# Pooled attention and feed-forward: softmax normalisation of a head pair's two steps in joint instructions of 576 columns

## The chip, the cores and the metric

The kernel runs on one core of one Trainium2 chip. The metric is the device time of one execution in microseconds (us), as the median of the runs. Engines are named as in the profile: PE is TensorE, PEld its weight loads, DVE VectorE, ACT ScalarE, POOL GpSimd, SP SyncE (DMA issue only).

## What is computed

Attention with the queries pooled by two, and then a feed-forward network on its output. In the reference (fp32; B 4, H 8, S 1152, D 64; 2304 tokens, model width 512, hidden width 2048), shortened:

```python
q_pool = q.reshape(B, H, S // 2, 2, D).mean(axis=3)
scores = np.matmul(q_pool, k.transpose(0, 1, 3, 2)) / np.sqrt(D)
scores = scores - np.max(scores, axis=-1, keepdims=True)
attn = np.exp(scores)
attn = attn / (np.sum(attn, axis=-1, keepdims=True) + 1e-09)
x = np.matmul(attn, v)            # heads side by side: 2304 x 512
h = x @ w_in
sp = np.log1p(np.exp(np.minimum(h, 20.0)))   # h itself where h > 20
out = (h * np.tanh(sp)) @ w_out
```

## The kernel before

The attention runs in 32 steps. A step is one batch, one pair of heads and one half of the pooled queries: 2 heads x 288 queries = 576 columns. Two steps that follow each other, an even and an odd one, are the two halves of the same head pair; "a pair" below means these two steps, 16 pairs in all. The keys are cut into nine chunks of 128. The work of several steps overlaps: one step's scores are made while an earlier step's exponentials and still earlier steps' normalisations are done.

In a step, QK (L164) makes the scores of a chunk in PSUM (tile `s`, two buffers), CP (L174, ScalarE) copies them to SBUF (`TA`, `TB`), MX and MXF (L185, L189, VectorE) take a running maximum (`rmax`). MT, TMAX and MB (L200, L206, L217) turn it into one maximum per query, spread over all partitions; SUB (L223, VectorE) subtracts it, EXP (L227, ScalarE) exponentiates. PV (L246) multiplies with the values into the PSUM tile `pv`, of which there is one; PVE (L257, ScalarE) copies it to SBUF (`pvs`), and the next step's first PV waits for that copy. For the denominator, ADD (L232 to L238) sums the exponentials of the chunks on GpSimd, three chunks of them by a DMA that adds (L236, `acc<-TB`), and FIN0 (L268) sums over the partitions with a matrix of ones into the PSUM tile `Sb`, whose value stands in all partitions.

The normalisation, which the change touches, follows, for steps 0 to 29, on 288 columns (each head on its 64 partitions). With s the sum: FLN (L273, ScalarE) makes ln(s), FEX (L276, ScalarE) r = exp(-ln s), FC (L280, ScalarE) e = -s, FE (L284, GpSimd) e = e r, FT (L288, ScalarE) e = 2 + e, which is one Newton step on r, FU (L299, GpSimd) `pvs` = `pvs` r, and FX (L303, GpSimd) writes e times `pvs` to `xT`, the input of the feed-forward part. Steps 30 and 31 are normalised by VectorE instead (LX).

The order of the instructions is written out by hand: tables FILL, STEP, PAIR and EDGE give each action a time, and the program sorts by it. STEP has one time for even and one for odd steps, counted in steps after the step's own start; FILL and EDGE hold those of the first and the last steps. An engine works through its instructions in this order and waits at each for its operands and its buffer. The rows of STEP for the actions of the change:

```python
            (FC, 3.4059, 3.6027),
            (FLN, 3.4296, 3.4470),
            (FEX, 3.5419, 3.4904),
            (FE, 3.6257, 3.7684),
            (FU, 4.1203, 3.8913),
            (FT, 4.3117, 3.9096),
            (FX, 4.8298, 4.4442),
```

The feed-forward part starts as the attention ends, at about 423 us, and holds TensorE until the end.

Of the kernel before, what the change touches and what calls it, by code (L numbers as in the profile page):

```python
# [8 lines left out]
F32 = mybir.dt.float32  # L9
# [3 lines left out]
AF = mybir.ActivationFunctionType  # L13
ALU = mybir.AluOpType
# [9 lines left out]
def tile_pooled_attention_then_winograd_ffn(ctx: ExitStack, tc: tile.TileContext, q, k, v, moe_w_in, moe_w_out, out, outT):  # L24
    nc = tc.nc
    B, H, S, D = SHAPE
    SQ = S // 2
    NT, DM = B * SQ, out.shape[1]
    DFF = moe_w_out.shape[0]
    P = 128  # L30
# [3 lines left out]
    HQ = SQ // 2  # L34
# [15 lines left out]
    pe, dve, act, pool, sp = nc.tensor, nc.vector, nc.scalar, nc.gpsimd, nc.sync  # L50
# [4 lines left out]
    one, eps = (cst[:, n:n + 1] for n in range(2))  # L55
    xT = const.tile([P, NP, NT], F32, name="xT")

    steps = [(b, hp, hf) for b in range(B) for hp in range(NP) for hf in range(2)]
# [4 lines left out]
    def open_pool(name, bufs, side="left", space=bass.MemoryType.SB):  # L63
        shut[name] = ExitStack()
        pools[name] = shut[name].enter_context(
            tc.tile_pool(name=name, bufs=bufs, side=side, space=space, reuse_waits="tile")
        )
        return pools[name]
# [3 lines left out]
    if True:  # L72
# [7 lines left out]

        p1 = open_pool("p1", 1)
        p2 = open_pool("p2", 2)
        p3 = open_pool("p3", 3)
        pqk = open_pool("pqk", 2)
        pre = open_pool("pre", 1)
        wraw_p = open_pool("wraw", 2, side="right")
# [63 lines left out]
        rmaxs, Mbs, pvs, pvn, accs = {}, {}, {}, {}, {}  # L150
# [89 lines left out]
        def PV(i, c):  # L240
# [4 lines left out]
            for j in range(2):  # L245
# [5 lines left out]
                    stop=(pvn[i] == NC),  # L251
                )

        def PVE(i):
            ps = pvs[i]
            pvs[i] = p3.tile([P, HQ], F32, tag="pvs", name=f"pvs{i}")
            act.copy(pvs[i], ps[:, 0:HQ])  # L257

        fin = {}

# [8 lines left out]
            fin[i] = Sb[:, 0:HQ]  # L269

        def FLN(i):
            fin[i, "r"] = p2.tile([P, HQ], F32, tag="rs", name=f"rs{i}")
            act.activation(fin[i, "r"], fin[i], AF.Ln, bias=eps)  # L273

        def FEX(i):
            act.activation(fin[i, "r"], fin[i, "r"], AF.Exp, scale=-1.0)  # L276

        def FC(i):
            fin[i, "e"] = p2.tile([P, HQ], F32, tag="es", name=f"es{i}")
            act.activation(fin[i, "e"], fin[i], AF.Copy, bias=-1e-9, scale=-1.0)  # L280

        def FE(i):
            e = fin[i, "e"]
            pool.tensor_tensor(e, e, fin[i, "r"], ALU.mult)  # L284

        def FT(i):
            e = fin[i, "e"]
            act.activation(e, e, AF.Copy, bias=2.0, scale=1.0)  # L288

        def LX(i):  # L290

            b, hp, hf = steps[i]
            r = p2.tile([P, HQ], F32, tag="rs", name=f"rs{i}")
            dve.tensor_scalar(r, fin.pop(i), 1e-9, None, ALU.add)
            dve.reciprocal(r, r)
            dve.tensor_tensor(xT[:, hp, b * SQ + hf * HQ:b * SQ + (hf + 1) * HQ], r, pvs.pop(i), ALU.mult)

        def FU(i):
            pool.tensor_tensor(pvs[i], pvs[i], fin[i, "r"], ALU.mult)  # L299

        def FX(i):
            b, hp, hf = steps[i]
            pool.tensor_tensor(  # L303
                xT[:, hp, b * SQ + hf * HQ:b * SQ + (hf + 1) * HQ], fin[i, "e"], pvs.pop(i), ALU.mult
            )

        QHP = (1,)
        pieces = [(2 * fp + j % 2, j // 2) for fp in range(NFP) for j in range(4)]
# [291 lines left out]
        ps, sv = {}, {}  # L600
# [142 lines left out]
        for n, u in enumerate(units):  # L743
            if u[0] == 0:
                banks[u] = ("b", "a", "c") if n % 2 else ("a", "b", "c")
            else:
                x, y, z = banks[units[n - 1]]
# [3 lines left out]
        XD = (0, 1, 2, 3)  # L751
        BYREC = (NS - 2, NS - 1,)
        GONE = [(i, fn) for i in BYREC for fn in (FLN, FEX, FC, FE, FT, FU, FX)]
        def close(*names):
            for n in names:
                shut[n].close()
# [15 lines left out]
            open_pool("ps2", 1, side="right", space=PSUM)  # L772

        def reuse_rest():
            close("p3", "p2", "p1")
            open_pool("wf", 1)
            open_pool("pad", 1).tile([P, 16], F32, name="pad")
            open_pool("xt", 1)
            open_pool("ev", 2)
            open_pool("sx", 2)  # L780
            open_pool("x3", 1)

        def reuse_lead():
# [139 lines left out]
            (2.0890, QK, 2, 6),  # L923
            (2.1220, SUB, 1, 2),
            (2.1370, PVE, 0),
            (2.1370, QK, 2, 7),
            (2.1570, ADD, 1, 0),
# [56 lines left out]
            (3.1610, QK, 3, 7),  # L984
            (3.2030, SUB, 2, 2),
            (3.2062, PVE, 1),
            (3.2157, QK, 3, 8),
            (3.2287, ADD, 2, 0),
# [11 lines left out]
            (3.4400, QK, 4, 0),  # L1000
            (3.4460, ADD, 1, 3),
            (3.4540, FLN, 0),
            (3.4840, SUB, 2, 3),
            (3.4960, QK, 4, 1),
            (3.5080, CP, 4, 0),
            (3.5510, FC, 0),
            (3.5510, PV, 2, 4),
            (3.5739, CP, 4, 1),
            (3.6030, QK, 4, 2),
            (3.6170, FEX, 0),  # L1010
            (3.6200, load_k, 3),
            (3.6350, MX, 4, 1),
            (3.6510, MT, 3),
            (3.6650, FE, 0),
            (3.6710, CP, 4, 2),
            (3.7010, QK, 4, 3),
# [28 lines left out]
            (4.1590, QK, 4, 7),  # L1045
            (4.2010, SUB, 3, 2),
            (4.2030, PVE, 2),
            (4.2130, QK, 4, 8),
            (4.2257, CP, 4, 7),
# [3 lines left out]
            (4.3040, MX, 4, 7),  # L1053
            (4.3130, PV, 3, 1),
            (4.3230, FLN, 1),
            (4.3520, PV, 3, 3),
            (4.3550, FC, 1),
            (4.3580, MX, 4, 8),
            (4.3780, EXP, 3, 2),
# [3 lines left out]
            (4.4300, load_q, 4),  # L1063
            (4.4390, QK, 5, 0),
            (4.4650, FEX, 1),
            (4.4820, SUB, 3, 3),
            (4.4930, FU, 0),
            (4.4940, QK, 5, 1),
            (4.5180, CP, 5, 0),
# [20 lines left out]
            (4.9120, QK, 5, 5),  # L1090
            (4.9210, ADD, 2, 4),
            (4.9210, FT, 0),
            (4.9350, MX, 5, 4),
            (4.9450, EXP, 4, 0),
# [6 lines left out]
            (5.0880, CP, 5, 6),  # L1101
            (5.0920, MX, 5, 5),
            (5.1170, FX, 0),
            (5.1192, PV, 3, 8),
            (5.1300, EXP, 4, 1),
            (5.1460, MX, 5, 6),
            (5.1678, QK, 5, 7),
            (5.1790, FE, 1),
            (5.2000, SUB, 4, 2),
            (5.2157, QK, 5, 8),  # L1110
# [20 lines left out]
            (5.5480, PV, 4, 4),  # L1131
            (5.5600, CP, 6, 1),
            (5.5810, FU, 1),
            (5.6000, QK, 6, 2),
            (5.6030, FT, 1),
            (5.6200, load_k, 4),
            (5.6297, MX, 6, 1),
            (5.6460, FX, 1),
            (5.6480, MT, 5),
            (5.6680, CP, 6, 2),  # L1140
# [615 lines left out]
            (10.1622, A_g, 1, 1),  # L1756
            (10.4532, FIN0, 30),
            (10.5378, LX, 30),
            (10.6934, ADD, 31, 3),
            (10.9320, A_gh, 2, 0),  # L1760
# [10 lines left out]
            (13.1756, A_gh, 2, 1),  # L1771
            (13.3311, split_l, 3, 1),
            (13.5491, LX, 31),
            (13.7245, O_, 1, 0),
            (14.2248, reuse_rest),
            (14.3971, XS, 0, "T1"),
            (14.5382, split_l, 4, 3),
# [789 lines left out]
        for u in units:  # L2567
            if 2 <= u[1] <= NFP - 2:
                for t, fn, *a in STEADY[u[0] > 0]:
                    a = (4 * u[1] + a[0], a[1]) if fn is conv else (u, *a)  # L2570
# [46 lines left out]
```

## Time and profile before

| | |
|---|---|
| median of 3 runs | 785.08 us (784.74 to 788.81) |
| profiled execution | 784.51 us, span 782.7 us |
| granted TensorE clock, mean | 0.993 of full speed |
| busy share of the span | PE 98%, DVE 87%, ACT 82%, POOL 84% |
| chain that ended last | PE 86%, DVE 3%, ACT 3%, DMA 3%, POOL 2% |
| attention | about 0 to 423 us |

The span reaches from the first to the last instruction of the profiled execution. An engine's busy share is an average over the attention and the feed-forward part, which have different loads, so the stretches have to be looked at apart. Ends of matrix multiplications are modelled, so a busy PE need not be PE at its peak.

### The profile page before, as it was taken

To read this page: it belongs to the slowest core of one execution; us is meant where nothing else is said; L and a number is where in the kernel's file an instruction comes from. 1 tells how busy PE (TensorE), PEld (TensorE's weight loads), DVE (VectorE), ACT (ScalarE), POOL (GpSimd) and SP (SyncE) were. 2 spreads that over 40 slices of the span, in tenths; PEclk is the share of its full clock that TensorE was granted. 3 is DMA by queue.
4 is the path that set the end of the run, shared out by engine and by line. 5 is a ranking of instruction groups with operands and counts; after the bars stand their busy time and mean duration, and the time that the engine had idled before them with its cause. 6 is when DMAs were issued, how large, how long until landed. Compare 5 with 4: busy or idle time off the path is not lost.

```text
span 782.7 us, 14324 instructions
## 1 busy us (share of the span) xinstructions
PE 767.4 (98%) x5123; PEld 558.1 (71%) x5123; DVE 680.6 (87%) x959; ACT 642.1 (82%) x1110; POOL 654.3 (84%) x505
## 2 busy tenths in 40 slices
PE   7999999999999999999999999999999999999998
PEld 5454555545555454555557988899899999999998
DVE  5999999999999999999976778877778889587876
ACT  6999999999999999999885887777677687877762
POOL 4679988989889898988887598886788899998884
PEclk9899999999999999999999999999999999999999
DMA  7556575565755656455432788874664232254242
GB/s 269 166 152 142 176 176 116 143 151 138 181 111 149 152 137 170 116 148 116 111 69 46 241 277 290 284 257 172 192 210 151 95 121 69 95 172 142 95 132 101
DMA packets 44470, 121.90 MB, mean 156 GB/s; under 512 B 4592, under 2 KB 16368, under 8 KB 44400
## 3 DMA queue, kind: packets, MB, share of 16 engines
q1 hardware_dynamic: 34608, 71.45, 27.5%
q0 software_dynamic: 4608, 28.31, 18.4%
q10 hardware_dynamic: 5184, 21.24, 8.0%
q8 instruction: 40, 0.66, 0.3%
q14 instruction: 30, 0.25, 0.1%
HBM read 70.65 MB, written 22.02 MB: 118 GB/s over the span
## 4 chain that ended last, share of the span: by engine, by line
PE 86%; DVE 3%; ACT 3%; DMA 3%; POOL 2%; issue 1%; SPq 0%; ACTq 0%; DVEq 0%; POOLq 0%
PE s L164 20%; PE pv L246 17%; PE ma L616 11%; PE O L727 8%; PE OAy L678 7%; PE mc L616 6%; PE O L678 6%; PE mb L616 3%; PE Sb L268 2%; DMA acc<-TB 2%; PE mt L200 2%; PE h L433 1%; PE Mb L217 1%; PE OZ L710 1%; POOL acc L238 1%
## 5 line engine op out<-in xcount | busy, mean ns | idle before, releaser
L164 PE MATMUL s<-qT,kT 64*128 64x288 f32 x1152 | 205.4, 454 | 4.0 <-ACT TB L174 1.8
L164 PEld LDWEIGHTS s<-qT,kT 64*128 64x128 f32 x1152 | 94.0, 189 | 99.8 <-DVE rmax L185 24.9
L174 ACT COPY TA<-s 128x576 f32<-128x576 f32 x192 | 117.9, 638 | 22.9 <-PE s L164 16.5
L223 DVE TENSOR_TENSOR TA<-TA,Mb 128x1152 f32<-128x1152 f32 x96 | 128.9, 1347 | 1.9 <-PE Mb L217 1.0
L227 ACT ACTIVATE TA<-TA 128x1152 f32<-128x1152 f32 x96 | 112.8, 1176 | 4.1 <-DVE TA L223 3.6
L246 PE MATMUL pv<-TA,vn 128*64 128x288 f32 x768 | 115.2, 422 | 0.8 <-ACT TA L227 0.8
L232 POOL TENSOR_TENSOR acc<-TA 128x1152 f32<-128x1152 f32 x32 | 85.0, 2656 | 36.2 <-PE s L164 19.1
L185 DVE TENSOR_TENSOR rmax<-s,rmax 128x576 f32<-128x576 f32 x128 | 93.3, 749 | 2.1 <-ACT TB L174 1.8
L238 POOL TENSOR_TENSOR acc<-acc 128x576 f32<-128x576 f32 x64 | 91.9, 1436 | 3.9 <-DMA acc<-TB 2.6
L246 PEld LDWEIGHTS pv<-TA,vn 128*64 128x64 f32 x768 | 47.2, 137 | 48.5 <-issue 9.7
L691 DVE TENSOR_TENSOR xT<-xT,OAy 128x384 f32<-128x384 f32 x104 | 54.7, 548 | 11.9 <-PE OAy L678 11.6
L223 DVE TENSOR_TENSOR TB<-TB,Mb 128x1728 f32<-128x1728 f32 x32 | 62.2, 1944 | 0.0
L246 PE MATMUL pv<-TB,vn 128*64 128x288 f32 x384 | 61.3, 415 | 0.0
L174 ACT COPY TB<-s 128x576 f32<-128x576 f32 x96 | 59.8, 654 | 1.8 <-PE s L164 1.7
L598 POOL TENSOR_TENSOR wbl<-wS,wbh 128x1024 fp32r<-128x1024 f32 x20 | 49.5, 2476 | 5.8 <-ACT wbh L594 5.8
L227 ACT ACTIVATE TB<-TB 128x1728 f32<-128x1728 f32 x32 | 52.7, 1648 | 0.0
L185 DVE TENSOR_TENSOR rmax<-s,TA 128x576 f32<-128x576 f32 x64 | 48.3, 755 | 3.8 <-ACT TA L174 3.7
L234 POOL TENSOR_TENSOR acc<-TA 128x576 f32<-128x576 f32 x32 | 45.6, 1424 | 2.5 <-ACT TA L227 2.3
L246 PEld LDWEIGHTS pv<-TB,vn 128*64 128x64 f32 x384 | 24.0, 136 | 25.2 <-issue 11.9
L598 POOL TENSOR_TENSOR wal<-wS,wah 128x768 fp32r<-128x768 f32 x19 | 36.8, 1936 | 3.3 <-ACT wah L594 3.1
L598 POOL TENSOR_TENSOR woal<-wO,woah 128x1024 fp32r<-128x1024 f32 x13 | 31.4, 2415 | 7.9 <-ACT woah L594 6.4
L620 ACT COPY s<-ma 128x384 f32<-128x384 f32 x44 | 21.2, 482 | 20.2 <-PE ma L616 20.2
(305 smaller groups left out, 2241.3 us busy)
## 6 DMA issues: line engine op xcount, KB each, us to landing
acc<-TB POOLq DMA_DIRECT2D x32, 864.0 KB, 6.4
ri<-in_moe_w_in_dram SPq DMA_DIRECT2D x16, 512.0 KB, 4.6
ro<-in_moe_w_out_dram SPq DMA_DIRECT2D x16, 512.0 KB, 4.2
qn<-in_q_dram ACTq DMA_DIRECT2D x12, 576.0 KB, 5.0
kT<-in_k_dram ACTq DMA_DIRECT2D x12, 576.0 KB, 3.8
vn<-in_v_dram ACTq DMA_DIRECT2D x12, 576.0 KB, 4.1
wS<-sumsh SPq DMA_DIRECT2D x12, 512.0 KB, 4.0
wO<-sumso SPq DMA_DIRECT2D x13, 384.0 KB, 4.4
```

Of the source, the lines that this page charges most:

```text
L164: pe.matmul(s[:, j, 0:HQ], kT[64 * j:64 * j + 64, c], qT[64 * j:64 * j + 64, hf], start=True, stop=True,)
L174: act.copy(T(i, c), ss[i, c])
L185: dve.tensor_tensor(ss[i, c] if c == FOLD else r, ss[i, c], x, ALU.max)
L223: dve.tensor_tensor(x, x, Mbs[i].unsqueeze(1).to_broadcast([P, w, W]), ALU.subtract)
L227: act.activation(x, x, AF.Exp, scale=0.0625)
L232: pool.tensor_tensor(accs[i][:, 0:2], T(i, 0, 2), T(i, 2, 4), ALU.add)
L238: pool.tensor_tensor(accs[i][:, 0], accs[i][:, 0], accs[i][:, n - 2], ALU.add)
L246: pe.matmul(pvs[i][64 * j:64 * j + 64, 0:HQ], vn[:, j, c, :], T(i, c)[:, j], start=(pvn[i] == 1), stop=(pvn[i] == NC),)
L598: (dve if e == "dve" else pool).tensor_tensor(l, w_part(u, q), f32(h), ALU.subtract)
L616: pe.matmul(o, a, b, start=(new and m == 0), stop=(last and m == len(seq) - 1), skip_group_check=True)
L678: pe.matmul(o, x, y, start=(n == 0 and i not in CHAIN_O[1:]), stop=(n == 2 and i not in CHAIN_O[:3]), skip_group_check=True)
L727: pe.matmul(o, x, y[:, f], start=(f == 0 and m == 0), stop=(f == 1 and m == 2))
```

## The change

Instead of one tile of 288 columns for each step, `pvs`, `rs` and `es` become tiles of 2 x 288 columns for each pair; `half_of` picks a step's half. PVE, FLN and FC still run for each step and write their half. FEX, FE, FT, FU and FX run only for the odd step of a pair, on all 576 columns, and do nothing for the even step. The tables are the same, so the joint instruction stands where the odd step's stood. `pvs` had three buffers of one step and has two of a pair now; `rs` and `es` had two of one step and have two of a pair. 15 pairs are normalised so: 15 x 3 products of GpSimd and 15 x 2 operations of ScalarE fall away, and as many are twice as long.

```diff
-        p3 = open_pool("p3", 3)
...
+        def half_of(x, i):
+            return x[i // 2][:, i % 2]
+
+        pvx, rsx, esx = {}, {}, {}
+
         def PVE(i):
-            ps = pvs[i]
-            pvs[i] = p3.tile([P, HQ], F32, tag="pvs", name=f"pvs{i}")
-            act.copy(pvs[i], ps[:, 0:HQ])
+            ps = pvs.pop(i)
+            if i // 2 not in pvx:
+                pvx[i // 2] = p2.tile([P, 2, HQ], F32, tag="pvs", name=f"pvs{i // 2}")
+            act.copy(half_of(pvx, i), ps[:, 0:HQ])
...
         def FLN(i):
-            fin[i, "r"] = p2.tile([P, HQ], F32, tag="rs", name=f"rs{i}")
-            act.activation(fin[i, "r"], fin[i], AF.Ln, bias=eps)
+            if i // 2 not in rsx:
+                rsx[i // 2] = p2.tile([P, 2, HQ], F32, tag="rs", name=f"rs{i // 2}")
+            act.activation(half_of(rsx, i), fin[i], AF.Ln, bias=eps)
+
+        def FC(i):
+            if i // 2 not in esx:
+                esx[i // 2] = p2.tile([P, 2, HQ], F32, tag="es", name=f"es{i // 2}")
+            act.activation(half_of(esx, i), fin[i], AF.Copy, bias=-1e-9, scale=-1.0)
 
         def FEX(i):
-            act.activation(fin[i, "r"], fin[i, "r"], AF.Exp, scale=-1.0)
-
-        def FC(i):
-            fin[i, "e"] = p2.tile([P, HQ], F32, tag="es", name=f"es{i}")
-            act.activation(fin[i, "e"], fin[i], AF.Copy, bias=-1e-9, scale=-1.0)
+            if i % 2:
+                r = rsx[i // 2]
+                act.activation(r, r, AF.Exp, scale=-1.0)
 
         def FE(i):
-            e = fin[i, "e"]
-            pool.tensor_tensor(e, e, fin[i, "r"], ALU.mult)
+            if i % 2:
+                e = esx[i // 2]
+                pool.tensor_tensor(e, e, rsx[i // 2], ALU.mult)
 
         def FT(i):
-            e = fin[i, "e"]
-            act.activation(e, e, AF.Copy, bias=2.0, scale=1.0)
+            if i % 2:
+                e = esx[i // 2]
+                act.activation(e, e, AF.Copy, bias=2.0, scale=1.0)
+
+        def FU(i):
+            if i % 2:
+                x = pvx[i // 2]
+                pool.tensor_tensor(x, x, rsx[i // 2], ALU.mult)
+
+        def FX(i):
+            if i % 2:
+                b, hp, _ = steps[i]
+                x = xT[:, hp, b * SQ:(b + 1) * SQ].rearrange("p (a b) -> p a b", a=2)
+                pool.tensor_tensor(x, esx.pop(i // 2), pvx.pop(i // 2), ALU.mult)
```

The order of TensorE's and of VectorE's instructions is the same before and after. GpSimd's, first: a stretch from the middle of the attention, from a step's first sum of exponentials (L232) to the DMA sum (L236). The line numbers of the changed kernel differ: L284, L303 and L299 of before are FE, FX and FU, and L294, L310 and L304 are the same after; the last row but one is the sum that FIN0 waits for. Before:

```order
L232 TENSOR_TENSOR acc_2409<-TA_158 128x1152
L238 TENSOR_TENSOR acc_2289<-acc_2289 128x576
L234 TENSOR_TENSOR acc_2409<-TA_158 128x576
L284 TENSOR_TENSOR es_2449<-es_2449,rs_2434 128x288
L303 TENSOR_TENSOR xT<-es_2305,pvs_2154 128x288
L299 TENSOR_TENSOR pvs_2284<-pvs_2284,rs_2434 128x288
L238 TENSOR_TENSOR acc_2289<-acc_2289 128x576
L236 DMA acc_2409<-TB_159 128x1728
```

The same stretch after:

```order
L231 TENSOR_TENSOR acc_2580<-TA_155 128x1152
L237 TENSOR_TENSOR acc_2463<-acc_2463 128x576
L233 TENSOR_TENSOR acc_2580<-TA_155 128x576
L294 TENSOR_TENSOR es_2479<-es_2479,rs_2482 128x576
L304 TENSOR_TENSOR pvs_2334<-pvs_2334,rs_2482 128x576
L237 TENSOR_TENSOR acc_2463<-acc_2463 128x576
L235 DMA acc_2580<-TB_156 128x1728
```

FE and FU are an odd step's and have become joint; FX was an even step's and is gone from here. In the other step of the pair, FX is the joint one and FE and FU are gone.

ScalarE's, second: from an odd step's FT (L288 before, L299 after) to PVE (L257 before, L262 after), the copy that frees `pv`. Before:

```order
L288 ACTIVATE es_3659<-es_3659 128x288
L227 ACTIVATE TA_158<-TA_158 128x1152
L174 COPY TA_158<-s_5_3706 128x576
L174 COPY TB_159<-s_6_3717 128x576
L227 ACTIVATE TA_158<-TA_158 128x1152
L257 COPY pvs_3736<-pv_3621 128x288
```

After:

```order
L299 ACTIVATE es_3415<-es_3415 128x576
L226 ACTIVATE TA_155<-TA_155 128x1152
L173 COPY TA_155<-s_5_3599 128x576
L173 COPY TB_156<-s_6_3610 128x576
L226 ACTIVATE TA_155<-TA_155 128x1152
L262 COPY pvs_3504<-pv_3518 128x288
```

Nothing has moved here; FT has 576 columns instead of 288, and PVE, still of one step, comes behind it.

## Rows read from the trace of the kernel before

**Rows 1.** Busy us of each engine in one stretch, clock, DMA.

```profile
core 0: us, PE busy (x) PEld busy (x) DVE busy (x) ACT busy (x) POOL busy (x), PEclk, DMA share, GB/s
200.00:240.00 40.00, 40.00 (x313) 20.82 (x311) 39.29 (x42) 37.49 (x62) 36.03 (x30) 1.00 0.60 156
```

**Rows 2.** Waits, 40 to 400 us: total us, times, longest.

```profile
PEld s L164 <- DVE rmax L185: 22.5, 56, 0.6
...
POOL acc L232 <- ACT TA L227: 14.6, 12, 1.5
```

**Rows 3.** Chain of work that ended last: start us, us, engine, output, line.

```profile
198.03 2.09 PE pv L246 x16
...
222.63 2.09 PE pv L246 x16
```

**Rows 4.** Instructions by line and shape, 0 to 405 us: busy us, mean ns.

```profile
L174 ACT COPY TA<-s 128x576 f32<-128x576 f32 x192 | 117.9, 638 | 22.9 <-PE s L164 16.5 <-POOL xT L303 4.2 <-DVE rmax L185 1.9
...
L227 ACT ACTIVATE TA<-TA 128x1152 f32<-128x1152 f32 x93 | 109.3, 1177 | 2.1 <-DVE TA L223 1.8
...
L227 ACT ACTIVATE TB<-TB 128x1728 f32<-128x1728 f32 x31 | 51.1, 1648 | 0.0
...
L138 POOL TENSOR_TENSOR qT<-qn 128x576 f32<-128x576 f32 x15 | 25.4, 1695 | 1.8 <-DMA qn<-in_q_dram 1.8
...
L276 ACT ACTIVATE rs<-rs 128x288 f32<-128x288 f32 x30 | 13.4, 447 | 0.4
L288 ACT ACTIVATE es<-es 128x288 f32<-128x288 f32 x28 | 12.9, 462 | 0.0
```

**Rows 5.** Timeline of GpSimd, tight step: start us, us, instruction.

```profile
214.08 1.42 POOL L234 TENSOR_TENSOR acc<-TA 128x576 f32<-128x576 f32 x1
215.46 0.79 POOL L284 TENSOR_TENSOR es<-es,rs 128x288 f32<-128x288 f32 x1
216.21 0.80 POOL L303 TENSOR_TENSOR xT<-es,pvs 128x288 f32<-128x288 f32 x1
216.97 0.80 POOL L299 TENSOR_TENSOR pvs<-pvs,rs 128x288 f32<-128x288 f32 x1
217.73 1.41 POOL L238 TENSOR_TENSOR acc<-acc 128x576 f32<-128x576 f32 x1
```

**Rows 6.** Timeline of all engines, same step: Sb, PVE and pv.

```profile
220.11 0.20 PEld L268 LDWEIGHTS Sb<-acc,cst 128*64 128x64 f32 x4 [0.38 <-issue]
...
221.83 0.42 ACT L257 COPY pvs<-pv 128x288 f32<-128x288 f32 x1
...
222.56 0.44 PEld L246 LDWEIGHTS pv<-TA,vn 128*64 128x64 f32 x6 [0.39 <-ACT pvs L257]
```

**Rows 7.** Timeline of GpSimd and TensorE, steps 3 to 6; the page's DMA issues.

```profile
78.52 0.80 POOL L299 TENSOR_TENSOR pvs<-pvs,rs 128x288 f32<-128x288 f32 x1
79.56 0.80 POOL L303 TENSOR_TENSOR xT<-es,pvs 128x288 f32<-128x288 f32 x1 [0.24 <-ACT es L288]
...
83.17 0.88 POOL L236 DMA_DIRECT2D acc<-TB  x1
...
90.41 1.41 POOL L238 TENSOR_TENSOR acc<-acc 128x576 f32<-128x576 f32 x1
...
94.66 1.41 POOL L238 TENSOR_TENSOR acc<-acc 128x576 f32<-128x576 f32 x1
...
97.08 0.71 PE L268 MATMUL Sb<-acc,cst 128*64 128x288 f32 x4
...
acc<-TB POOLq DMA_DIRECT2D x32, 864.0 KB, 6.4
```

**Rows 8.** Timeline of GpSimd and TensorE around one late DMA.

```profile
337.34 1.42 POOL L238 TENSOR_TENSOR acc<-acc 128x576 f32<-128x576 f32 x1 [1.57 <-DMA acc<-TB]
...
343.82 0.70 PE L268 MATMUL Sb<-acc,cst 128*64 128x288 f32 x4 [0.63 <-POOL acc L238]
```

**Rows 9.** Chain of work that ended last, end of the attention.

```profile
393.55 0.33 ACT es L288
...
407.98 0.67 ACT es L288 x2
```

More of the change, by code (lines that the diff above doesn't have):

```diff
@@ L290, in LX @@
         def LX(i):
             b, hp, hf = steps[i]
-            r = p2.tile([P, HQ], F32, tag="rs", name=f"rs{i}")
+            if i // 2 not in rsx:
+                rsx[i // 2] = p2.tile([P, 2, HQ], F32, tag="rs", name=f"rs{i // 2}")
+            r = half_of(rsx, i)
             dve.tensor_scalar(r, fin.pop(i), 1e-9, None, ALU.add)
             dve.reciprocal(r, r)
-            dve.tensor_tensor(xT[:, hp, b * SQ + hf * HQ:b * SQ + (hf + 1) * HQ], r, pvs.pop(i), ALU.mult)
-        def FU(i):
-            pool.tensor_tensor(pvs[i], pvs[i], fin[i, "r"], ALU.mult)
@@ L301, in FX @@
[L301 to L305, printed above, removed]
+            dve.tensor_tensor(xT[:, hp, b * SQ + hf * HQ:b * SQ + (hf + 1) * HQ], r, half_of(pvx, i), ALU.mult)
         QHP = (1,)
@@ L774, in reuse_rest @@
         def reuse_rest():
-            close("p3", "p2", "p1")
+            close("p2", "p1")
             open_pool("wf", 1)
```

## The prediction

> **What bounds the kernel now.** I read four views in this order: busy time by stretches, the waits, the chain of work that ended last, and the timeline around the products that the change touches. They have to answer one question: do ScalarE and GpSimd, the two engines that the change relieves, ever hold up the other two?
>
> In 40 us of steady attention TensorE is busy 40.00, VectorE 39.29, ScalarE 37.49 and GpSimd 36.03 [rows 1]. Everything is nearly full, so busy time alone does not name the bound. The chain of work does: it stays on TensorE all through the attention, and the block of sixteen pv records that opens each step starts at 198.03 and, two steps later, at 222.63 [rows 3]. That is 24.60 us for a head pair, 12.30 a step. The waits say what paces TensorE: the longest is for `rmax`, VectorE's running maximum, 22.5 us in 56 cases, 0.4 each [rows 2]; the score tile has two buffers, so QK waits until MX has read the chunk before the last. So TensorE and VectorE drive each other in a closed loop. GpSimd, by contrast, stands idle before its first sum of a step: 14.6 us in 12 cases, 1.2 each, waiting for ScalarE's exponentials [rows 2]. Time given back to GpSimd ahead of that point only makes this idle time longer.
>
> One could also read [rows 1] as TensorE alone being full, with 40.00 of 40. [...]
>
> **The prices.** *ScalarE.* An operation on 288 columns takes 447 ns (FEX) or 462 ns (FT) [rows 4]. None on 576 columns reads and writes SBUF in this trace, so I bound it. From above, two of today's operations end to end. From the exponentials: 1177 ns at 1152 columns and 1648 at 1728, so 471 for 576 more, and 1177 - 471 = 706 ns for 576. From below, the copy of 576 columns out of PSUM, 638 ns. I take 706, the same kind of operation. A pair then saves 2 x 447 - 706 = 188 ns and 2 x 462 - 706 = 218 ns, 0.41 us, over 15 pairs 6.1 us of ScalarE's time. But the joint operation stands in the odd step's place, and there it is 0.26 (FEX) and 0.24 us (FT) longer than what stood there.
>
> *GpSimd.* Its instructions follow each other: FE starts at 215.46, FX at 216.21, FU at 216.97, the last sum at 217.73, so a product on 288 columns costs 0.76 us of its queue; the sum on 576 columns at 214.08 costs 1.38 [rows 5]. Dearest of 576 columns is the pooling of q, 1695 ns [rows 4]; cheapest would be 0.76, nothing for the second half. I take 1.38, since the sum also reads two tiles of contiguous columns, as the products will. Each product that goes frees 0.76, each joint one adds 0.62 in its place. A pair saves 3 x (1.52 - 1.38) = 0.42 us, 6.3 over 15 pairs.
>
> **Where these land.** *Sums, the tight step.* Between GpSimd's idle time and the sum that Sb waits for stand FE, FX and FU [rows 5]. FE and FU are an odd step's and become joint; FX is an even step's and goes: +0.62 + 0.62 - 0.76 = +0.48. The sum ends at 217.73 + 1.41 = 219.14 and Sb starts at 220.11 [rows 5, 6], 0.97 later. So half of that margin goes and TensorE does not wait: 0. In the other step FX grows and FE goes, -0.14: the sum and the DMA behind it come a little sooner: 0. FU of an even step, which goes as well, stood just ahead of the idle time: 0.
>
> *The copy of pv.* FT of an odd step stands four ScalarE operations ahead of PVE, which frees the one PSUM bank for the next step's pv. PVE ends at 221.83 + 0.42 = 222.25 and pv starts at 222.56, a margin of 0.31 [rows 6]. FT pushes PVE back by 0.24 if nothing between has slack. 0.07 is left, about what a hand-over takes: 0. This is the thinnest place of the sum; behind PVE wait pv, then QK, MT and with them VectorE. FEX of an odd step is 0.26 longer, but FT of the even step, 0.33 of the queue by its like in [rows 9], went just ahead of it: 0.
>
> *The start, once.* Around 80 us FU and FX of step 1 are neighbours. FU at 78.52 becomes joint and ends its turn at 79.90, 0.34 after the 79.56 at which FX started (it waited 0.24 for FT, and that wait is now covered). FX adds 0.62, so the DMA sum at 83.17 is issued 0.96 later, at 84.13 [rows 7]. It takes 6.4 us to land [rows 7], so the next sum starts at 90.53 instead of 90.41. Ahead of that step's last sum stand FE and FU of step 3, both joint: +1.24. The sum at 94.66 comes at 94.66 + 0.12 + 1.24 = 96.02 and ends at 97.43, while Sb started at 97.08 [rows 7]: **+0.4 us**.
>
> *The late DMA, once.* One DMA sum landed late: GpSimd waited 1.57 us for it at 337.34, and TensorE then 0.63 for Sb at 343.82 [rows 8]. Here no margin is left, so the +0.48 of the tight step shows, less 0.14 from the earlier issue: **+0.3 us** if the transfer is late again.
>
> *The end of attention, once.* There ScalarE is on the chain. FT at 393.55 becomes joint: +0.24. The two FT at 407.98, 0.67 together, become one of about 0.60 [rows 9]: -0.07. Together **+0.2 us**. The feed-forward part has no instruction of the change.
>
> **The sum.** The profiled execution took 784.51 us (span 782.7 and 1.8 around it), 0.57 below the median of the runs. 784.51 + 0.4 + 0.3 + 0.2 = 785.4. I forecast **785.4 us**: no change, within the 0.5% (3.9 us) that a measurement of this kernel can tell.
>
> **The rivals.** *ScalarE paces the step after all (faster).* For it: ScalarE is busy 37.49 of 40. Then all of its saving arrives: 784.5 - 6.1 = 778.4. Against it: TensorE's longest wait is for VectorE, and the step repeats to the hundredth. To be faster by 0.5%, two thirds of the saving must arrive. Chance 0.05.
>
> *The joint products hold up Sb (slower).* The margin of 0.97 is used up when 2p - 3 x 0.76 exceeds it, p being the queue time of a joint product: from p = 1.62. At the 1.70 of the dearest row the sum comes 1.12 later, Sb 0.15 late, in 14 pairs 2.1 us; the start and the late DMA add 2 x 0.32 + 2 x 0.32 = 1.3. That gives 785.4 + 3.4 = 788.8; beyond 1.72 it is slower by over 0.5%. For it: 1695 ns was measured on these columns. Against it: that row reads strided columns and the next instruction starts before it has ended. Chance 0.12, half of it beyond 0.5%.
>
> *The joint FT holds up pv (slower).* If it saved nothing, it would add 0.46 instead of 0.24, and pv would come 0.46 - 0.31 = 0.15 late plus a hand-over, about 0.2; in 14 pairs 2.8 us, 788.2. It decides from 0.31 on. Against it: the slope of the exponentials. Chance 0.09, 0.03 beyond 0.5%.
>
> *Nothing arrives anywhere.* The late DMA does not come again and the start hides: 784.51 - 0.63 = 783.9. Chance 0.16, within 0.5%.
>
> **How the numbers follow.** The forecast has the remaining 0.58. Faster by over 0.5%: 0.05. Slower: 0.06 + 0.03 = 0.09. Within: 0.86. The range goes down past the case in which nothing arrives, 783.9, by the 0.3 between the two closer runs (784.74 and 785.08), to 783.6, and up almost to the dearest product: 783.6 to 788.6. It leaves out the ScalarE rival and the end of the GpSimd one, about 0.15.
>
> **What would show it.** In the changed profile: POOL's products on 576 columns near 1.4 us and ScalarE's near 0.7; ScalarE and GpSimd each about 6 us less busy, TensorE and VectorE as before; the pv blocks still 24.60 us apart per pair; Sb some 0.5 us behind its sum in the tight step, not 0.97; short waits of TensorE for Sb near 97 and, if the DMA is late, 344 us. Pairs shorter than 24.6 would refute the reading that VectorE and TensorE pace the step; pairs longer by 0.1 to 0.2, with TensorE waiting for `pvs` or `acc`, would mean that one of the two margins was too small.

## The result and the profile after

| | before | after |
|---|---|---|
| median, run side by side on one chip | 783.86 us (22 runs) | 788.06 us (22 runs) |
| ratio, with its 95% interval | | 1.0054 (1.0038 to 1.0070) |
| profiled execution, span and mean granted clock | 782.7 us, 0.993 | 783.3 us, 1.000 |

The changed kernel is slower by 4.2 us; its interval, 0.38% to 0.70%, lies around the 0.5% that was drawn as the limit of "no change". The two profiled spans are only 0.6 us apart, but the clock of the first 40 us and of the stretch from 360 to 400 us was lower in the profile before (0.91 and 0.96) than in the one after (1.00 in both), so the two are compared by the length of a pair, in stretches where both show 1.00.

The length of a pair. In the timeline of the changed kernel I take two blocks that occur once a step on TensorE, MT and the sixteen pv matmuls; the chain of waits of this profile can be followed back only to 423.03 us, so it does not serve here.

```profile
190.34 0.65 PE L199 MATMUL mt<-identr,rmax 64*128 64x64 f32 x10
198.16 2.16 PE L245 MATMUL pv<-TA,vn 128*64 128x288 f32 x16
202.87 0.65 PE L199 MATMUL mt<-identr,rmax 64*128 64x64 f32 x10
...
215.23 0.65 PE L199 MATMUL mt<-identr,rmax 64*128 64x64 f32 x10
223.05 2.16 PE L245 MATMUL pv<-TA,vn 128*64 128x288 f32 x16
```

The same blocks before:

```profile
190.37 0.65 PE L200 MATMUL mt<-identr,rmax 64*128 64x64 f32 x10
...
202.67 0.65 PE L200 MATMUL mt<-identr,rmax 64*128 64x64 f32 x10
...
214.97 0.65 PE L200 MATMUL mt<-identr,rmax 64*128 64x64 f32 x10
```

pv is 24.89 us apart, where [rows 3] had 24.60. By MT the pair's two steps were 12.30 and 12.30 and are 12.53 and 12.36: one step has lost 0.23, the other 0.055. This repeats in eleven pairs, 11 x 0.285 = 3.1 us. The start (below) adds 0.36, and the end of the attention about 0.2. Of the 4.2 us measured (3.0 to 5.5 by the interval) 3.7 are thus found.

The prices. Groups by line and shape, 0 to 405 us, against [rows 4, 5]: busy us and mean ns of one.

```profile
L294 POOL TENSOR_TENSOR es<-es,rs 128x576 f32<-128x576 f32 x14 | 20.4, 1454 | 0.0
L304 POOL TENSOR_TENSOR pvs<-pvs,rs 128x576 f32<-128x576 f32 x14 | 20.1, 1434 | 0.0
...
L289 ACT ACTIVATE rs<-rs 128x576 f32<-128x576 f32 x15 | 10.3, 689 | 0.4
L299 ACT ACTIVATE es<-es 128x576 f32<-128x576 f32 x14 | 9.8, 701 | 0.0
```

ScalarE's operations take 689 and 701 ns where 706 was taken. The steady stretch, against [rows 1], and the waits from 40 to 400 us, against [rows 2]:

```profile
200.00:240.00 40.00, 39.69 (x305) 19.91 (x303) 39.02 (x43) 37.20 (x58) 34.36 (x25) 1.00 0.60 153
```

```profile
POOL acc L231 <- ACT TA L226: 27.3, 13, 3.0
PEld s L163 <- DVE rmax L184: 24.6, 55, 0.7
...
DVE m L205 <- PE mt L199: 6.6, 28, 0.9
...
PE s L163 <- DVE rmax L184: 2.0, 12, 0.3
```

GpSimd is relieved (36.03 to 34.36 busy of 40) and spends it waiting for ScalarE's exponentials: 27.3 us where it was 14.6. TensorE was never idle in this stretch (40.00) and now is (39.69). The last row says for whom: 12 times, once a pair, its matmul QK itself waits for `rmax`, VectorE's running maximum.

Why `rmax` is late. Timeline of the step whose FT became joint; L299 is the joint FT, L222 VectorE's subtraction, the copy of L173 that of score tile s_5, the first maximum of L184 at 220.88 that of the same tile, L262 PVE.

```profile
218.57 0.70 ACT L299 ACTIVATE es<-es 128x576 f32<-128x576 f32 x1
...
219.15 1.17 ACT L226 ACTIVATE TA<-TA 128x1152 f32<-128x1152 f32 x1
219.40 1.34 DVE L222 TENSOR_TENSOR TA<-TA,Mb 128x1152 f32<-128x1152 f32 x1
...
220.21 0.65 ACT L173 COPY TA<-s 128x576 f32<-128x576 f32 x1
220.35 0.20 PEld L273 LDWEIGHTS Sb<-acc,cst 128*64 128x64 f32 x4 [0.38 <-issue]
...
220.88 1.42 DVE L184 TENSOR_TENSOR rmax<-s,rmax 128x576 f32<-128x576 f32 x2
...
221.70 1.42 PE L163 MATMUL s<-qT,kT 64*128 64x288 f32 x8 [0.16 <-DVE rmax L184]
...
222.32 0.42 ACT L262 COPY pvs<-pv 128x288 f32<-128x288 f32 x1
```

The same instructions before:

```profile
218.31 0.46 ACT L288 ACTIVATE es<-es 128x288 f32<-128x288 f32 x1
...
219.14 1.34 DVE L223 TENSOR_TENSOR TA<-TA,Mb 128x1152 f32<-128x1152 f32 x1
...
219.71 0.65 ACT L174 COPY TA<-s 128x576 f32<-128x576 f32 x1
...
220.40 1.41 DVE L185 TENSOR_TENSOR rmax<-s,rmax 128x576 f32<-128x576 f32 x2
...
221.23 1.40 PE L164 MATMUL s<-qT,kT 64*128 64x288 f32 x8
```

From FT's start to the copy of s_5 it was 1.40 us and is 1.64: the joint FT pushes it back by the forecast 0.24. From VectorE's subtraction to its next maximum it was 1.26 and is 1.48. Before, that subtraction ended at 220.48 and the copy at 220.36, and the maximum started at 220.40 (neighbours on VectorE can overlap, here by 0.08). Now the subtraction ends at 220.74 and VectorE stands still until 220.88, 0.02 after the copy has ended at 220.86. VectorE waits for ScalarE's copy although both only read the same PSUM tile; the program puts the copy first. The margin had been 0.04, and half of it is used up by the 0.02 between the copy's end and the maximum's start, so nearly all of the 0.24 arrives. The margin of PVE, on which the prediction spent its attention, is unchanged: PVE ends at 222.74 and pv starts at 223.05, 0.31 later as in [rows 6].

The start, against [rows 7]: GpSimd and TensorE, step 6.

```profile
89.49 1.42 POOL L237 TENSOR_TENSOR acc<-acc 128x576 f32<-128x576 f32 x1 [1.03 <-DMA acc<-TB]
...
94.99 1.41 POOL L237 TENSOR_TENSOR acc<-acc 128x576 f32<-128x576 f32 x1
...
96.45 0.70 PE L273 MATMUL Sb<-acc,cst 128*64 128x288 f32 x4 [0.64 <-POOL acc L237]
```

Sb waits for the sum, as forecast. That step takes 12.72 us instead of 12.30; the step before it is 0.06 shorter, so the start costs 0.36 (forecast 0.4).

### The profile page after: what moved, and what is told of

Same layout as the page of the kernel before. It is cut to its first block, busy times and chain, and to the rows that moved or that the text cites. A ratio compares the mean times of both kernels' runs of the same rounds, so it can differ in the third digit from the quotient of the medians.

```text
span 783.3 us, 14245 instructions
## 1 busy us (share of the span) xinstructions
PE 764.4 (98%) x5123; PEld 553.9 (71%) x5123; DVE 681.3 (87%) x959; ACT 640.6 (82%) x1080; POOL 648.3 (83%) x460
## 5 line engine op out<-in xcount | busy, mean ns | idle before, releaser
L163 PEld LDWEIGHTS s<-qT,kT 64*128 64x128 f32 x1152 | 92.1, 187 | 103.4 <-DVE rmax L184 27.1
L173 ACT COPY TA<-s 128x576 f32<-128x576 f32 x192 | 117.5, 638 | 27.6 <-PE s L163 25.7
L222 DVE TENSOR_TENSOR TA<-TA,Mb 128x1152 f32<-128x1152 f32 x96 | 128.8, 1347 | 0.9 <-PE Mb L216 0.8
L184 DVE TENSOR_TENSOR rmax<-s,rmax 128x576 f32<-128x576 f32 x128 | 93.3, 750 | 3.0 <-ACT TB L173 0.7
L222 DVE TENSOR_TENSOR TB<-TB,Mb 128x1728 f32<-128x1728 f32 x32 | 62.2, 1944 | 0.0
L173 ACT COPY TB<-s 128x576 f32<-128x576 f32 x96 | 59.6, 653 | 0.3 <-PE s L163 0.2
L184 DVE TENSOR_TENSOR rmax<-s,TA 128x576 f32<-128x576 f32 x64 | 48.2, 753 | 3.8 <-ACT TA L173 3.5
```

The source lines that it names most:

```text
L163: pe.matmul(s[:, j, 0:HQ], kT[64 * j:64 * j + 64, c], qT[64 * j:64 * j + 64, hf], start=True, stop=True,)
L173: act.copy(T(i, c), ss[i, c])
L184: dve.tensor_tensor(ss[i, c] if c == FOLD else r, ss[i, c], x, ALU.max)
L222: dve.tensor_tensor(x, x, Mbs[i].unsqueeze(1).to_broadcast([P, w, W]), ALU.subtract)
```

## The experiments

Two theories stood after the profile. **The copy of s_5**: the joint FT costs 0.23 a pair because VectorE's maximum waits for the ScalarE copy that FT pushes back, and the missing even FEX costs the other 0.055. **The copy of pv**: the prediction's rival, by which FT holds up PVE and pv. The copy theory says that the place of ScalarE's work decides, not its amount. Each ratio is to runs of the kernel before taken beside it; the pair is MT to MT over two steps, from about 190 us on.

| kernel | median us (runs) | ratio (95%) | steps | pair |
|---|---|---|---|---|
| before | 783.86 (22) | | 12.30 / 12.30 | 24.60 |
| after | 788.06 (22) | 1.0054 (1.0038 to 1.0070) | 12.53 / 12.36 | 24.89 |
| `ft_behind_copy6` | 789.05 (5) | 1.0072 (1.0059 to 1.0086) | 12.66 / 12.35 | 25.01 |
| `fex_per_step` | 787.52 (6) | 1.0048 (1.0033 to 1.0062) | 12.53 / 12.30 | 24.83 |
| `extra_at_ft` | 785.89 (12) | 1.0034 (1.0021 to 1.0047) | 12.62 / 12.31 | 24.93 |
| `extra_behind_copy8` | 783.82 (12) | 1.0008 (0.9997 to 1.0018) | 12.30 / 12.30 | 24.60 |
| `ft_behind_copy8` | 786.14 (12) | 1.0020 (1.0006 to 1.0033) | 12.30 / 12.35 | 24.65 |
| `both_undone` | 785.81 (12) | 1.0020 (1.0003 to 1.0038) | 12.30 / 12.32 | 24.62 |
| `filler_for_fex` | 787.07 (1) | none | 12.54 / 12.35 | 24.89 |
| `two_products_joint` | 783.98 (11) | 0.9998 (0.9985 to 1.0011) | 12.30 / 12.30 | 24.60 |

The first four experiments were run together, beside 23 runs of the kernel before with a median of 783.19 us; the last four beside 29 with 784.1.

**`extra_at_ft`.** The kernel before, with one more ScalarE operation on 288 columns, on a scratch tile that nothing reads, behind FT in nine odd steps. Nothing else is changed.

```diff
+        def XT(i):
+            if i % 2 and 6 < i < 24:
+                act.copy(scr, one.to_broadcast([P, HQ]))
...
             (FT, 4.3117, 3.9096),
+            (XT, 4.3117, 3.9100),
```

> The kernel before, nothing joint, with one more ScalarE operation of 288 columns on a scratch tile right behind FT of the nine odd steps 7 to 23. It adds about 0.34 us of ScalarE's queue at the place where the joint FT added 0.24. Theory: the copy of chunk 5 and VectorE's maximum come 0.34 late, those nine pairs take 24.60 + 0.33 = 24.93 us, 3.0 us more than before. Rival (the loss is in the joint products or in the tiles of a pair): the pairs stay at 24.60.

The pair grew by 0.33, nearly all of it in the step in which the extra operation runs (12.62). The waits of VectorE, 40 to 400 us:

```profile
DVE rmax L186 <- ACT TA L175: 2.4, 10, 0.3
```

The timeline of one such step:

```profile
222.45 0.64 ACT L175 COPY TA<-s 128x576 f32<-128x576 f32 x1
...
223.12 1.42 DVE L186 TENSOR_TENSOR rmax<-s,rmax 128x576 f32<-128x576 f32 x2 [0.23 <-ACT TA L175]
...
223.94 1.42 PE L165 MATMUL s<-qT,kT 64*128 64x288 f32 x8 [0.23 <-DVE rmax L186]
224.56 0.42 ACT L258 COPY pvs<-pv 128x288 f32<-128x288 f32 x1
...
225.29 1.43 PE L247 MATMUL pv<-TA,vn 128*64 128x288 f32 x10
```

Here the profile names the idle time (in the changed kernel it gave none for the 0.14 from 220.74 to 220.88): VectorE waits 0.23 for ScalarE's copy of s_5, and behind it QK waits 0.23 for VectorE. pv starts 0.31 after PVE's end (224.98), so it is not what waits. An operation of ScalarE that has nothing to do with the normalisation makes the same loss. The maximum starts at 223.12, 0.03 after the copy's end at 223.09. What an overlap of these two reads would do, no run here shows.

**`extra_behind_copy8`.** The same operation in the same steps, but behind the copy of s_8.

```diff
             (FT, 4.3117, 3.9096),
+            (XT, 4.3117, 4.2820),
```

> The kernel before with the same extra ScalarE operation in the same nine pairs, but behind the copy of chunk 8, where ScalarE waits 0.4 us for TensorE soon after. Theory (the place counts, not the work): pairs of 24.60 us, time as before. Rival (ScalarE's total work paces the step): 24.9 and 3 us more, as with the extra operation behind FT.

The pairs stay at 24.60 and the time is the same within the noise, 1.0008 (0.9997 to 1.0018). The place decides, not the work. One step of this profile, before the pairs of the table, takes 12.58, and one of `extra_at_ft` in the same place 12.57; why is open.

**`ft_behind_copy6`.** The changed kernel, with the joint FT behind the copy of s_6 (and so in the first and last steps).

```diff
-            (FT, 4.3117, 3.9096),
+            (FT, 4.3117, 4.0900),
```

> The changed kernel, with the joint FT issued two copies later on ScalarE, behind the copy of chunk 6 instead of ahead of the exponentials and the copy of chunk 5; PVE still comes as late as in the changed kernel. Theory (the joint FT delays the copy of chunk 5, and VectorE's running maximum of that chunk waits for this copy): VectorE's wait ahead of it goes, and a pair takes 24.66 us instead of 24.88, so about 2.5 us less than the changed kernel (11 of the pairs are moved), some 1.5 us more than the kernel before. Rival (the delayed PVE holds up the next step's pv): PVE is as late as before the move, a pair stays at 24.83 to 24.88 and the time is the changed kernel's.

A miss: 25.01 us a pair, worse than the changed kernel. Timeline of ScalarE, VectorE and TensorE:

```profile
218.12 1.35 DVE L222 TENSOR_TENSOR TA<-TA,Mb 128x1152 f32<-128x1152 f32 x1
...
219.51 1.17 ACT L226 ACTIVATE TA<-TA 128x1152 f32<-128x1152 f32 x1
...
220.38 0.76 PE L163 MATMUL s<-qT,kT 64*128 64x288 f32 x4
...
221.19 0.64 ACT L173 COPY TB<-s 128x576 f32<-128x576 f32 x1
...
221.72 0.69 ACT L299 ACTIVATE es<-es 128x576 f32<-128x576 f32 x1
...
223.36 0.39 ACT L262 COPY pvs<-pv 128x288 f32<-128x288 f32 x1
...
223.80 2.16 PE L245 MATMUL pv<-TA,vn 128*64 128x288 f32 x16 [0.20 <-ACT pvs L262]
...
224.32 0.76 DVE L184 TENSOR_TENSOR rmax<-s,rmax 128x576 f32<-128x576 f32 x1 [0.27 <-ACT TB L173]
```

The wait for the copy of s_5 is gone, but the same one has appeared two tiles on, at s_7 (0.27). I had expected ScalarE to run ahead by the slot that FT left. It hardly could: the exponential starts 0.04 after VectorE's subtraction has ended (219.51 after 219.47), and the copy of s_6 0.05 after the modelled end of its QK (221.19 after 221.14). So nearly the whole FT, not the 0.24 by which it had grown, stood ahead of PVE and of the copy of s_7. Here pv did wait for PVE as well (0.20), and started 0.05 after its end: the rival's mechanism exists, from a larger delay on.

**`ft_behind_copy8`.** The same, behind the last copy of the step.

```diff
-            (FT, 4.3117, 3.9096),
+            (FT, 4.3117, 4.2820),
```

> The changed kernel with the joint FT issued behind the copy of chunk 8, so behind all copies that VectorE's running maximum waits for in this step. The run with FT behind the copy of chunk 6 showed that FT's whole length counts where the copy ahead of it waits for TensorE, and that the maximum of chunk 7 then waits for its copy. Theory: no maximum waits here, only the 0.05 of ScalarE's extra wait is left, a pair takes 24.66 us instead of 24.88, 2.4 us less than the changed kernel. Rival (a joint FT costs wherever it stands): 24.83 to 25.0.

24.65 as expected: the 0.23 is gone, the 0.055 has stayed. That the run is still 1.0020 slower (0.5 to 2.6 us by the interval) fits 11 x 0.055 = 0.6 us and the 0.36 of the start. One DMA sum is late in its profile, as one was in the profile before (a step of 12.97 here and of 12.71 there); the interval does not separate these.

**`fex_per_step`.** The changed kernel, with FEX for each step on its half.

```diff
         def FEX(i):
-            if i % 2:
-                r = rsx[i // 2]
-                act.activation(r, r, AF.Exp, scale=-1.0)
+            r = half_of(rsx, i)
+            act.activation(r, r, AF.Exp, scale=-1.0)
```

> The changed kernel with FEX again once for each step on 288 columns; FE, FT, FU, FX stay joint. Theory (0.05 us of a pair's 0.28 come from an extra wait of ScalarE for its own earlier work at the copy of chunk 2, which appeared when FEX of the even step went): the odd 0.05 goes, a pair takes 24.83 us, 0.6 us less than the changed kernel over 12 pairs. Rival (all of it hangs on FT): 24.88, no difference.

The step of 12.36 is 12.30 again, the other has stayed at 12.53. So the two losses are separate, and the small one belongs to the even FEX that is no longer there. Its place in the timeline is ScalarE's copy of s_2 in the even step, with the QK that it follows. The changed kernel, and `fex_per_step`:

```profile
202.28 0.76 PE L163 MATMUL s<-qT,kT 64*128 64x288 f32 x4
...
203.14 0.64 ACT L173 COPY TA<-s 128x576 f32<-128x576 f32 x1 [0.75 <-PE s L163]
```

```profile
202.28 0.76 PE L163 MATMUL s<-qT,kT 64*128 64x288 f32 x4
...
203.09 0.64 ACT L173 COPY TA<-s 128x576 f32<-128x576 f32 x1 [0.46 <-PE s L163]
```

The copy starts 0.86 after QK with the even FEX gone and 0.81 with it. In the program built from the changed kernel, this copy has to wait for ScalarE's own earlier exponential as well as for QK. In the kernel before and in `fex_per_step` it waits for QK alone, and the even FEX, two places ahead, has a wait for ScalarE's own work that comes later than that exponential.

**`filler_for_fex`.** Is it this wait, or that ScalarE stands idle there? The changed kernel with an operation of 256 columns on a scratch tile where the even FEX stood.

```diff
+        def XT(i):
+            if i % 2 == 0 and 6 <= i < 24:
+                act.copy(scr, one.to_broadcast([P, 256]))
...
             (FEX, 3.5419, 3.4904),
+            (XT, 3.5419, 3.4904),
```

> The changed kernel with a ScalarE operation of 256 columns on a scratch tile where FEX of the even step stood (steps 6 to 22). ScalarE's queue is as full there as before the change, but the extra wait of the copy of chunk 2 for ScalarE's own earlier work stays. Theory (it is this wait that costs 0.05): the step after stays at 12.35 us. Rival (it is the changed timing of the copies around the gap): back to 12.30, as with FEX for each step.

The timeline:

```profile
201.71 0.41 ACT L289 COPY scr<-cst 128x256 f32<-128x256 f32 x1
...
202.35 0.76 PE L164 MATMUL s<-qT,kT 64*128 64x288 f32 x4
...
203.20 0.64 ACT L174 COPY TA<-s 128x576 f32<-128x576 f32 x1 [0.55 <-PE s L164]
```

0.85 after QK, and 12.35 a step: filling the idle time changes nothing, so idleness is not the cause. In its program the copy still has the wait for ScalarE's own exponential. That this wait costs the 0.055 fits all three kernels but is no row of any profile; it was not taken away by itself, so the cause of this smaller loss is argued and not shown.

**`both_undone`.** FEX for each step and FT behind the copy of s_8 (the two edits above together).

> The changed kernel with the joint FT behind the copy of chunk 8 and FEX once for each step again; GpSimd's products stay joint. Theory: both losses are gone, a pair takes 24.60 us, if FEX of the even step, which FT now pushes back by up to 0.25, does not make the copy of chunk 1 late; if it does, 24.65 to 24.75. Time 0.5 to 1.5 us above the kernel before. Rival (the joint products hold up Sb): 24.7 and more, with TensorE waiting for the sum on GpSimd.

24.62: both losses are gone but for 0.02, whose place I did not test. At the start Sb of step 6 waits for its sum as in the changed kernel (0.75 us), since the three products are joint here too; that step and the next take 12.82 and 12.51. The start and the 0.02 together make about 0.8 of the 1.7 us that this kernel is slower (0.2 to 3.0 by the interval).

**`two_products_joint`.** Only FU and FX joint; FE and ScalarE's FEX and FT for each step as before.

```diff
         def FE(i):
-            if i % 2:
-                e = esx[i // 2]
-                pool.tensor_tensor(e, e, rsx[i // 2], ALU.mult)
+            e = half_of(esx, i)
+            pool.tensor_tensor(e, e, half_of(rsx, i), ALU.mult)
...
         def FT(i):
-            if i % 2:
-                e = esx[i // 2]
-                act.activation(e, e, AF.Copy, bias=2.0, scale=1.0)
+            e = half_of(esx, i)
+            act.activation(e, e, AF.Copy, bias=2.0, scale=1.0)
```

> The changed kernel with only FU and FX joint; FE, FT and FEX run once for each step, so ScalarE's instructions are those of before. Theory (the loss is ScalarE's): pairs of 24.60 us, at the start 0.4 us or less more, time 0 to 0.6 us above the kernel before. Rival (GpSimd's joint products or the tiles of a pair cost): 24.7 to 24.9 and 1.5 to 4 us.

0.9998 (0.9985 to 1.0011), pairs of 24.60. These two joint products on GpSimd cost nothing in the steady part, and gain nothing; with FE joint too, `both_undone` was within 0.02 of it. At the start, FE of step 3 is single again, which takes 0.62 from the sum of step 6 that Sb waits for: GpSimd's sum and TensorE's Sb.

```profile
95.25 1.42 POOL L237 TENSOR_TENSOR acc<-acc 128x576 f32<-128x576 f32 x1
...
96.73 0.70 PE L273 MATMUL Sb<-acc,cst 128*64 128x288 f32 x4
```

Sb has no wait here, and the step takes 12.31. No version was faster than the kernel before by more than the noise.

## Why the prediction was wrong in its main term

**Bound and prices: right in the main.** That VectorE and TensorE pace the step fits every run (a maximum that started 0.22 later made its step 0.23 longer), and work taken from GpSimd goes into its idle time (27.3 us after 14.6). The joint operations cost what was forecast (706 against 689 and 701 ns, 1.38 us of GpSimd's queue against 1.36, as FE starts at 215.73 and FU behind it at 217.09), and Sb starts 0.47 behind its sum in the tight step (220.35 after 219.88), as forecast. The row of 1695 ns was set aside as one that reads strided columns; by the kernel it reads two runs of 288 contiguous columns, so that ground did not hold, though the price did. ScalarE's saving was put too high: 6.1 us came from durations, but neighbours on ScalarE overlap. FT, 0.46 long, took 0.35 of its queue before (218.31 to 218.66) and, 0.70 long, takes 0.58 now (218.57 to 219.15); a pair saves 2 x 0.35 - 0.58 = 0.12 there, not 0.22, and over the whole span ScalarE is only 642.1 - 640.6 = 1.5 us less busy.

**The step that failed: "The copy of pv ... 0".** It saw that FT pushes ScalarE's queue back by 0.24, asked who waits for that, and named PVE alone ("behind PVE wait pv, then QK, MT and with them VectorE"). That margin of 0.31 is there still, to the hundredth. But the queue between FT and PVE holds two copies, and VectorE's maximum of s_5 waits for the first of them, with a margin of 0.04. So 0.23 of the 0.24 went into the loop that paces the step. The text also called PVE "the thinnest place of the sum"; the thinnest was one that no row of it showed, because [rows 2] lists waits that occurred and a margin of 0.04 leaves none. The list that [rows 2] is taken from did have a sign: ScalarE's copies release the weight loads of QK 44 times, `rmax` 56 times.

```profile
PEld s L164 <- ACT TA L174: 19.6, 44, 0.8
```

The prediction passed over this row. `extra_at_ft` and `extra_behind_copy8` show the step that failed: the same operation costs 0.33 ahead of that copy and nothing behind the last one.

**A term that was missing.** That an instruction falls away was put at no cost. Without the even FEX a pair is 0.055 longer, 0.6 us over eleven pairs.

**The once-only terms.** The start was right (0.4 against 0.36, with the wait for Sb where it was placed). The late DMA did not come again in the profile after. It did in `ft_behind_copy8`, where the three products are joint too: Sb waited 0.90 us (at 344.24) against 0.63 before, 0.27 more where 0.3 was forecast, though the two transfers need not have been equally late. The end is 0.2 by comparison: from MT at 377.08 to MT at 402.26 the changed kernel takes 25.18, the two kernels with the extra operation, which leave these steps as before, 24.96, all three at a granted clock of 1.00 there.

**The sum.** Forecast + 0.9 us on the profiled execution; measured + 4.2. Nearly all of the difference is 11 x 0.285 = 3.1 us, of which 2.5 are in the term that was put at 0 and 0.6 in the one that was missing. The 788.06 lies inside the stated range, 783.6 to 788.6, and that is luck: the range reached so far up for the dearest price of GpSimd's products, and these cost what was forecast. Its last sign fits no better: it spoke of pairs longer by 0.1 to 0.2 with TensorE waiting for `pvs` or `acc`, and they are longer by 0.285 with TensorE waiting for `rmax`. Of the rivals, the joint FT in front of pv had the right instruction and, again by luck, nearly the right size (about 0.2 in 14 pairs, 788.2 us; measured were 0.23 in eleven). Its condition, a joint FT that saves nothing, did not come true, and it had the wrong wait: FT grew by 0.24, the gap from PVE to pv was 0.31, and pv did not wait. The rival that ScalarE paces the step had its sign wrong: ScalarE does reach into the loop, by where its work stands and not by how much it is, and so joining FT in its old place lost time. The joint products ahead of Sb cost what the sum had put, nothing in the steady part.

## What to carry to other kernels

Joining two operations saved work here (0.12 us of ScalarE's queue a pair for FT) but made the one that is left longer where it stands (0.70 us for 0.46). What that cost was decided by what stood behind it in its engine's queue: 0.23 us with the copy of s_5 behind it, nothing where it stood behind the copy of s_8. The margin to be read is that of the first such instruction that the pacing engine waits for, not of the last or of the best-known one. In this kernel two engines that read the same PSUM tile were such a pair (VectorE waited 0.23 us for ScalarE's copy in `extra_at_ft`), though neither gives the other any data. When an engine is not the bound, put its longer operations behind the last instruction that others wait for in the step: in this kernel even an added operation of 0.45 us cost nothing there (pairs of 24.60 us in `extra_behind_copy8`).

## What was unexpected of the hardware

An operation less was slower here: without the even FEX the copy two places behind it starts 0.86 us after the QK that it follows, with it 0.80 to 0.81, and an operation of 0.41 us in its place did not restore it (0.85). And VectorE's maximum started 0.02 to 0.03 us after the end of ScalarE's copy of the same tile (220.88 after 220.86, 223.12 after 223.09), so a hand-over between these two engines took hardly any time. Into TensorE it was longer, 0.05 from PVE to pv in `ft_behind_copy6` (223.80 after 223.75) and 0.06 from VectorE's maximum to QK in `extra_at_ft` (223.94 after 223.88), near the 0.07 that the prediction allowed without a row for it.
